# Order of two weight loads at the head of a decode kernel: the last 64 rows of wq ahead of the other 512

## The chip, the cores and the metric

The kernel runs on one core of one Trainium2 chip. The metric is the device time of one execution in microseconds (us). Profiles are single executions taken by the hardware profiler; positions in them are us from the start of the profiled span, which is some 1.8 us shorter than the device time (378.4 against 380.22 in the profiled run of before).

## The reference

One decode step of a transformer block, four sequences of one token, width 576:

```python
q = (layernorm(x) @ wq)                 # wq: 576 x 4096, 32 heads of 128
k, v = last 4096 positions of 16 cached heads, each used by two query heads
h  = x + softmax(q k / sqrt(128)) v @ wo
h2 = h + (relu(gate(ln(h))) * up(ln(h))) @ W_down     # hidden width 4608
```

The caches make up most of the traffic: 4 sequences x 16 cached heads, four heads to a tile, so 16 K tiles and 16 V tiles of 4 MB each. Inputs and output are bf16.

## The kernel before

All large loads are issued by SyncE, in one list, and go to one DMA queue. K and V tiles and the main part of wq share a ring of four 4 MB slots. A load waits only for the last reader of the cells that it overwrites.

```python
def main_rows(W):                       # 512 rows: 128 partitions x 32 KB, one run each
    return W[0:512, :].rearrange("(p r) n -> p (r n)", r=4)

def last_rows(W):                       # 64 rows: 128 partitions x 4 KB, 512 KB in one piece
    return W[512:576, :].rearrange("r (a n) -> (r a) n", a=2)

s = ring_slot()
wq_off = slot0 + s * TILE
place(("wq", 0), wq_off, TILE, "QMM",
      lambda e: e.dma_start(out=arena[:, wq_off:wq_off + TILE], in_=main_rows(A_wq)), key=f"slot{s}")
P.dma("sync", ("L", "wq", 1), lambda e: e.dma_start(out=pT[:, 0:2048], in_=last_rows(A_wq)), "d_wq1")
for g in range(NTILE):
    add_kv("K", g)
    if g >= 4:
        add_kv("V", g - 4)
# ... the last V tiles, wo, gate, up and down weights
```

The q projection takes the main part first (chunks 0 to 3) and the last rows as chunk 4, so the wait for the last rows is met late:

```python
def pe_q():
    for c in range(DC):                 # 5 chunks of the contraction
        ...
                deps = []
                if bk == g == 0:
                    deps = {0: [("L", "wq", 0), "xnT", "c_xnT"], 4: [("L", "wq", 1)]}.get(c, [])
```

What follows of q: two evictions, which are copies of matmul results out of TensorE's result memory (L407, L408; 2.43 and 2.42 us), then transposes on TensorE, and eight copies on ScalarE (L422) that spread q into the operand of the QK matmuls (L455). A K tile is first transposed in place by VectorE (L431, two halves). The fourth K tile takes the ring slot of wq, so its load waits for the q matmuls.

The down projection ends the kernel: groups of 18 matmuls (L713), the last of them as the last pieces of W_down land.

Of the kernel before, what the change touches and what calls it, by code (L numbers as in the profile page):

```python
# [122 lines left out]
def bass_sequential_preLN__sliding_block_cached__glu_gated_reglu__decode_kernel(  # L123
# [12 lines left out]
    with ExitStack() as es:  # L136
# [5 lines left out]
        P = Prog()  # L142
# [54 lines left out]
        pT = pp[:, 0:4096]  # L197
# [34 lines left out]
        def ring_slot():  # L232
            s = ring[0] % NSLOT
            ring[0] += 1
            return s
# [12 lines left out]
        def main_rows(W):  # L248
            return W[0:512, :].rearrange("(p r) n -> p (r n)", r=4)

        def last_rows(W):
            return W[512:576, :].rearrange("r (a n) -> (r a) n", a=2)

        s = ring_slot()
        wq_off = slot0 + s * TILE
        place(("wq", 0), wq_off, TILE, "QMM",
              lambda e: e.dma_start(out=arena[:, wq_off:wq_off + TILE], in_=main_rows(A_wq)), key=f"slot{s}")
        P.dma("sync", ("L", "wq", 1), lambda e: e.dma_start(out=pT[:, 0:2048], in_=last_rows(A_wq)), "d_wq1")
        for g in range(NTILE):
            add_kv("K", g)  # L260
            if g >= 4:
# [21 lines left out]
        for j in range(4):  # L283
            wd_off.append(off)
            for r0, r1 in ((0, 9),) if j < 3 else ((0, 6), (6, 8), (8, 9)):
                place(("wd", j, r0), off + r0 * D, (r1 - r0) * D, ("DOWN", 1),
                      lambda e, off=off, j=j, r0=r0, r1=r1: e.dma_start(  # L287
                          out=arena[:, off + r0 * D:off + r1 * D],
                          in_=B_W_down[j * 1152:(j + 1) * 1152, :].rearrange("(p r) n -> p (r n)", p=128)[:, r0 * D:r1 * D]))
# [18 lines left out]
                                                in_=c_qm[:, :, :].rearrange("p q (h j) -> p q h j", j=4),  # L308
# [4 lines left out]
                                                in_=to_v[:, :, :].rearrange("p n (k a) -> p n k a", a=4),  # L313
# [303 lines left out]
        for a in range(8):  # L617
            for n in range(2):
                for j in range(4):
# [4 lines left out]
                    else:  # L624
# [6 lines left out]
                                             in_=bass.AP(tensor=psb, offset=512 + 224, ap=[[4096, 128], [1, 64], [0, 2]])), ["part1"])  # L631
# [87 lines left out]
        for n in range(2):  # L719
            P.dma(("sync", "scalar")[n], ("O", n), lambda e, n=n: e.dma_start(  # L720
                out=orow[:, 288 * n:288 * n + 288], in_=bass.AP(tensor=out_sb, offset=32 * n * 288, ap=[[8 * 288, 4], [1, 288]])),
# [31 lines left out]
```

## Time and profile before

| what | value |
|---|---|
| time, median of the 3 runs | 380.82 us (380.12 to 381.21) |
| span of the profiled run | 378.4 us |
| moved | 159.76 MB, 422 GB/s on average |
| DMA's share of the chain of waits | 61% |

The page of before. The row of digits is the busy share of the 16 DMA engines in 40 equal slices of the span, in tenths (9 is 90% or more); the queue's line has packets, MB, and the share of 16 engines' span; the last line is the chain of work that ended last, by engine.

```profile
span 378.4 us, 2668 instructions
...
DMA  8999999999999999999999999999999999999994
...
DMA packets 6660, 159.76 MB, mean 422 GB/s; under 512 B 748, under 2 KB 888, under 8 KB 1528
...
q1 hardware_dynamic: 6632, 159.59, 98.4%
...
DMA 61%; PE 19%; DVE 15%; issue 4%; SPq 1%
```

The DMA engines are busy from end to end on one queue. The time is set by how early this stream opens, how fast it runs and how soon its slowest engine is through; compute is on the path only at the very end (the time is the last landing plus 5.06 to 5.20 us while the clock stays at 1.00, see *All together*). The chain's last line still gives PE and DVE 34%: they free the ring slots that later loads wait for (SyncE's K and V loads waited 251.9 us in total for the matmuls of L34). Those loads are issued behind a backlog (the shortest time from issue to landing of a K tile was 17.9 us, with a tile landing every 9.71 us), and the stream does not stop for them: the DMA digit is 9 in 38 of 40 slices.

The timeline of before, its opening. Columns: start, duration, engine and line, operation, tiles; in brackets the idle time before it and what ended it.

```profile
0.73 0.38 SPq L257 DMA_DIRECT2D sb_arena<-in_A_wq_dram  x1
...
1.18 0.41 SPq L258 DMA_DIRECT2D sb_pp<-in_A_wq_dram  x1
...
1.63 35.71 SPq L245 DMA_DIRECT2D sb_arena<-in_A_k_cache_dram  x5
...
12.98 0.62 PE L387 MATMUL psb<-sb_arena,sb_xnT 128*32 128x512 bf16 x4 [4.23 <-DMA sb_arena<-in_A_wq_dram]
...
17.06 2.43 ACT L407 CAST sb_pp<-psb 128x512 bf16<-128x512 f32 x1 [8.51 <-PE psb L387]
...
20.80 9.69 ACT L422 COPY sb_arena<-sb_q_keep 32x256 bf16<-32x256 bf16 x8
...
23.96 8.77 DVE L431 STREAM_TRANSPOSE sb_arena<-sb_arena 128x4096 f32<-128x4096 f32 x2 [2.38 <-DMA sb_arena<-in_A_k_cache_dram]
...
32.79 0.66 PE L455 MATMUL psb<-sb_arena 128*32 128x512 bf16 x4 [12.63 <-DVE sb_arena L431]
```

Read it as a race: the first QK matmul (32.79) was released by the transposes of the first K tile, while the q copies had ended at 20.80 + 9.69 = 30.49. So q had 2.3 us to spare.

The DMA issues of before, us from issue to landing in the last column:

```profile
sb_arena<-in_A_wq_dram SPq DMA_DIRECT2D x1, 4096.0 KB, 12.2
...
sb_pp<-in_A_wq_dram SPq DMA_DIRECT2D x1, 512.0 KB, 13.0
```

### The profile page before, as it was taken

The page shows a single profiled execution, that of the slowest core. Times are in us where ns is not written, and L with a number is a line of the kernel's source. Part 1 is how long each engine was busy: PE and PEld are TensorE (multiplying, and loading weights), DVE is VectorE, ACT ScalarE, POOL GpSimd, SP SyncE. Part 2 cuts the span into 40 slices and gives each one's busy share as a digit, 9 for nine tenths or more (in the row PEclk, how much of TensorE's full clock was granted, in tenths as well). Part 3 has the DMA queues.
Part 4 walks back from the last instruction along what each step waited for, and adds up shares of the span by engine and source line. Part 5 has one row for each costly group of instructions (what it writes and reads, how often), then busy time and mean ns, then how long its engine had stood idle before and what let it go on. Part 6 is the DMA issues. An engine that isn't in the chain of part 4 may idle for free.

```text
span 378.4 us, 2668 instructions
## 1 busy us (share of the span) xinstructions
PE 213.3 (56%) x1471; PEld 38.3 (10%) x703; DVE 230.6 (61%) x206; ACT 54.2 (14%) x89; POOL 21.9 (6%) x44
## 2 busy tenths in 40 slices
PE   0404443149919191739291935674746598876774
PEld 0000000001101010101010100010101010003322
DVE  3178989779392959593838777766568523343220
ACT  3192000301000113010101130101010500122010
POOL 8860000000000000000000000000000000000000
PEclk9955888759958697687788895968796988998689
DMA  8999999999999999999999999999999999999994
GB/s 333 443 441 429 414 433 440 443 426 416 435 434 443 423 421 436 436 440 419 423 436 436 436 423 429 435 436 433 423 429 438 429 436 423 441 421 422 416 426 190
DMA packets 6660, 159.76 MB, mean 422 GB/s; under 512 B 748, under 2 KB 888, under 8 KB 1528
## 3 DMA queue, kind: packets, MB, share of 16 engines
q1 hardware_dynamic: 6632, 159.59, 98.4%
q8 instruction: 8, 0.13, 0.1%
q14 instruction: 4, 0.03, 0.0%
q10 hardware_dynamic: 16, 0.01, 0.0%
HBM read 159.58 MB, written 0.00 MB: 422 GB/s over the span
## 4 chain that ended last, share of the span: by engine, by line
DMA 61%; PE 19%; DVE 15%; issue 4%; SPq 1%
DMA sb_arena<-in_A_k_cache_dram 52%; DVE sb_arena L431 13%; PE psb L34 11%; DMA sb_arena<-in_B_W_down_dram 9%; PE psb L455 4%; PE psb L519 3%; DVE sb_o_tmp L532 1%; DVE sb_pp L497 1%; PE psb L545 0%; PE psb L713 0%; SPq L245 0%; PE psb L486 0%; SPq L287 0%; DVE sb_fq L543 0%; DVE sb_out_sb L716 0%
## 5 line engine op out<-in xcount | busy, mean ns | idle before, releaser
L431 DVE STREAM_TRANSPOSE sb_arena<-sb_arena 128x4096 f32<-128x4096 f32 x32 | 140.7, 4429 | 63.8 <-DMA sb_arena<-in_A_k_cache_dram 63.8
L34 PE MATMUL psb<-sb_arena,sb_pp 128*128 128x512 bf16 x384 | 106.6, 387 | 0.0
L455 PE MATMUL psb<-sb_arena 128*32 128x512 bf16 x256 | 44.3, 639 | 107.3 <-DVE sb_arena L431 107.3
L519 PE MATMUL psb<-sb_arena,sb_pp 128*128 128x512 bf16 x128 | 50.2, 392 | 9.3 <-DVE sb_o_tmp L532 9.3
L34 PE MATMUL psb<-sb_arena 128*32 128x512 bf16 x256 | 45.1, 643 | 0.0
L529 ACT COPY sb_o_tmp<-psb 32x512 f32<-32x512 f32 x32 | 18.5, 577 | 182.8 <-PE psb L34 182.5
L532 DVE TENSOR_TENSOR sb_o_tmp<-psb,sb_fm 32x512 f32<-32x512 f32 x32 | 21.7, 678 | 18.6 <-PE psb L34 18.1
L455 PEld LDWEIGHTS psb<-sb_arena 128*32 128x32 bf16 x256 | 9.7, 118 | 150.0 <-DVE sb_arena L431 120.2
L519 PEld LDWEIGHTS psb<-sb_arena,sb_pp 128*128 128x128 bf16 x128 | 12.7, 99 | 115.0 <-issue 115.0
L536 DVE TENSOR_REDUCE sb_o_sel<-sb_o_tmp 128x128 f32<-128x512 f32 x16 | 17.7, 1104 | 0.5
L476 ACT ACTIVATE sb_pp<-psb,sb_stat 128x512 bf16<-128x512 f32 x8 | 5.4, 682 | 80.9 <-DVE sb_stat L471 80.9
L497 DVE TENSOR_SCALAR sb_pp<-psb,sb_m 128x512 bf16<-128x512 f32 x16 | 10.8, 738 | 4.6 <-PE psb L486 4.6
L329 POOL TENSOR_SCALAR_AFFINE_SELECT sb_toq<-sb_toq 128x128 f32<-128x128 f32 x16 | 12.6, 788 | 2.3
L500 ACT ACTIVATE sb_pp<-psb,sb_m 128x512 bf16<-128x512 f32 x16 | 9.8, 697 | 12.7 <-PE psb L486 12.7
L535 DVE TENSOR_TENSOR sb_o_tmp<-sb_o_tmp,sb_fm 64x512 f32<-64x512 f32 x16 | 11.0, 690 | 0.5
L422 ACT COPY sb_arena<-sb_q_keep 32x256 bf16<-32x256 bf16 x8 | 9.7, 1445 | 0.1
L545 PE MATMUL psb<-sb_fq,sb_toq 128*128 128x4 f32 x8 | 1.8, 301 | 12.2 <-DVE sb_fq L543 12.2
L486 PE MATMUL psb<-sb_pp,sb_to_v 128*32 128x256 bf16 x64 | 4.3, 403 | 6.0 <-DVE sb_pp L480 6.0
L480 DVE STREAM_TRANSPOSE sb_pp<-sb_pp 128x512 bf16<-128x512 bf16 x8 | 5.5, 712 | 3.4 <-ACT sb_pp L476 3.4
L408 DVE CAST sb_pp<-psb 128x512 bf16<-128x512 f32 x1 | 2.4, 2425 | 8.1 <-PE psb L387 8.1
L713 PE MATMUL psb<-sb_arena,sb_pp 128*32 128x288 bf16 x72 | 5.9, 319 | 2.6 <-DMA sb_arena<-in_B_W_down_dram 2.6
L684 DVE TENSOR_TENSOR sb_pp<-psb,sb_pp 128x384 bf16<-128x384 f32 x3 | 1.5, 551 | 8.4 <-PE psb L675 8.4
(126 smaller groups left out, 91.6 us busy)
## 6 DMA issues: line engine op xcount, KB each, us to landing
sb_arena<-in_A_k_cache_dram SPq DMA_DIRECT2D x16, 4096.0 KB, 26.0
sb_arena<-in_A_v_cache_dram SPq DMA_DIRECT2D x16, 4096.0 KB, 27.9
sb_arena<-in_A_wo_dram SPq DMA_DIRECT2D x1, 4608.0 KB, 26.3
sb_arena<-in_B_W_gate_dram SPq DMA_DIRECT2D x1, 4608.0 KB, 27.8
sb_arena<-in_A_wq_dram SPq DMA_DIRECT2D x1, 4096.0 KB, 12.2
sb_arena<-in_B_W_down_dram SPq DMA_DIRECT2D x3, 1296.0 KB, 31.9
sb_arena<-in_B_W_up_dram SPq DMA_DIRECT2D x1, 3456.0 KB, 28.8
sb_arena<-in_B_W_up_dram SPq DMA_DIRECT2D x1, 1152.0 KB, 31.2
```

The lines of the kernel that those rows point to most:

```text
L34: return e.add_instruction(mybir.InstMatmult(name=e.bass.get_next_instruction_name(), engine=mybir.EngineType.PE, ins=[e.lower_ap(rhs), e. ...
L329: pool(f"c_toq{q + 1}", lambda e, q=q: e.affine_select(out=toq[:, :, :, :], in_=toq[:, :, :, :], pattern=[[0, 16], [-32, 4], [-1, 2]], com ...
L422: act("QW", lambda e, i=i, q=q: e.copy(out=bass.AP(tensor=arena, offset=32 * i * AW + 2 * i + q, ap=[[AW, 32], [512, 16], [136, 4], [32, 4]]),
L431: dve(("TRA", g, w), lambda e: e.transpose(out=dst, in_=src), [("L", "K", g)] if w == 0 else [])
L455: fn = lambda e, out_=out_, lhsT=lhsT, rhs=rhs, start=start, stop=stop: e.matmul(out_, lhsT=lhsT, rhs=rhs, start=start, stop=stop, skip_gr ...
L497: dve(("EV", b, 1), lambda e, out_=out_, src=src, a=a: e.tensor_scalar(out=out_, in0=src, scalar1=m4[:, a:a + 1], scalar2=None, op0=ALU.mu ...
L500: act(("EV", b, 0), lambda e, out_=out_, src=src, a=a: e.activation(out=out_, in_=src, func=ACT.Copy, scale=m4[:, a:a + 1]), deps + (["c_m ...
L519: fn = lambda e, lhsT=lhsT, rhs=rhs, k=k, j=j: e.matmul(bank[2 + j], lhsT=lhsT, rhs=rhs, start=(k == 0), stop=(k == 7), skip_group_check=True)
L529: act(("OSC", g), lambda e, j=j: e.copy(out=o_tmp[32 * j:32 * j + 32, 0:512], in_=bank[2 + j][32 * j:32 * j + 32, :]), [("PV", g), ("OSEL" ...
L532: dve(("OSD", g), lambda e, j=j: e.tensor_tensor(out=ot(32 * j, 32), in0=bank[2 + j][32 * j:32 * j + 32, :].rearrange("p (t d) -> p t d", ...
L535: dve(("OS", g), lambda e: e.tensor_tensor(out=ot(64, 64), in0=ot(64, 64), in1=fmb(64, 64), op=ALU.mult), [("OSC", g)])
L536: dve(("OSEL", g), lambda e: e.tensor_reduce(out=o_sel[:, qd, b, :], in_=o_tmp[:, 0:512].rearrange("p (t d) -> p d t", d=DH), axis=AX.X, o ...
```

## The change

The load of the last 64 rows is issued ahead of the main part. The aim of such a change would be to have the small piece there before it is needed; nothing else differs, and the instructions of every engine but SyncE stand in the same order.

```diff
+        P.dma("sync", ("L", "wq", 1), lambda e: e.dma_start(out=pT[:, 0:2048], in_=last_rows(A_wq)), "d_wq1")
         s = ring_slot()
         wq_off = slot0 + s * TILE
         place(("wq", 0), wq_off, TILE, "QMM",
               lambda e: e.dma_start(out=arena[:, wq_off:wq_off + TILE], in_=main_rows(A_wq)), key=f"slot{s}")
-        P.dma("sync", ("L", "wq", 1), lambda e: e.dma_start(out=pT[:, 0:2048], in_=last_rows(A_wq)), "d_wq1")
         for g in range(NTILE):
```

## The prediction

> **What bounds the kernel.** The DMA stream. The page counts 159.76 MB over a span of 378.4 us, 422 GB/s on average, and its row of DMA digits is 9 in 38 of 40 slices. Nearly all is one queue (98.4% of 16 engines' span), fed by SyncE. The semaphore events of the loads show a 4 MB tile landing every 9.71 us, from 23.94 us (first K tile) to 326.47 us (last V tile). DMA holds 61% of the chain of waits. The four-slot ring keeps a backlog: the shortest time from issue to landing of a K tile is 17.9 us against some 9.7 us of transfer, so about 8 us of other loads stand before it even at the worst.
>
> **What the change does.** No instruction and no byte is removed or added. On SyncE's queue two neighbours swap: the 0.5 MB load of the last 64 rows (128 packets of 4 KB) goes before the 4 MB load of the other 512 rows (128 packets of 32 KB). Neither waits for anything, each has its own semaphore, and the first K tile is third in both orders.
>
> [...] the main part landed at 12.94 us, the small part at 14.21 (1.27 us later, its own transfer), the first K tile at 23.94.
>
> So now the small part should land at about 4 us and the main part at about 14.2, where the pair ended before. TensorE starts the q projection with the main part, at 12.98 us before; it should start at about 14.2. In before the small part landed under the first matmuls and cost no wait (its chunk started at 16.37), so nothing is won in return. All that follows moves by about 1.25 us, an estimate from these landings: q evictions from 17.06 to about 18.3, the end of ScalarE's eight q copies (9.69 us) from 30.49 to about 31.75.
>
> **How much is critical.** None. (1) The first QK matmul at 32.79 waits for the transposes of the first K tile (VectorE, 8.77 us from 23.96), not for the q copies: 2.3 us of slack, 1.25 used. (2) VectorE idles 2.38 us before that transpose; its small q operations end at about 22.8 instead of 21.6. (3) The fourth K load reuses the q weights' slot and waits for the q matmuls (13.8 us in the queue's waits); it goes from about 17.4 to 18.6 us, but the loads ahead of it last until 43.78.
>
> A second-order term is the start: the first 32 KB packets took 1.6 to 2.2 us instead of the later 1.21. With 4 KB packets first this may change by a few tenths, either sign; I put it at zero.
>
> **Prediction: 380.8 us**, 379.7 to 381.9 in 8 of 10 cases. Chances: faster by over 2%: 0.01; within 2%: 0.98; slower by over 2%: 0.01.
>
> **What would show the steps.** Right: the q matmuls wait about 1.25 us longer for the q weights; the first QK matmul still at 32.8, still released by the transpose; the first K tile landing within 0.4 us of 23.9, all later landings within 0.5 us; same bytes. Wrong: first QK released by ScalarE; a hole in the DMA rate in the first slices; a K landing shifted by over 1 us.
>
> **What would make it wrong.** If 4 KB packets at the very start run much slower than at 13 us[...], the whole stream shifts by that hole[...]. If the q copies slowed down, the 1 us of slack left could go; even then the backlog should absorb it.

The forecast's sum is the median of the three known runs of before, 380.82 us, plus nothing: every term, the second-order one of the start included, was put at zero.

## The result, and the profile after

| | before | after |
|---|---|---|
| median | 380.54 us (4 runs, 380.12 to 381.21) | 379.72 us (4 runs, 379.70 to 379.77) |
| span of the profiled run | 378.4 us | 377.9 us |

The ratio was 0.9977, with a 95% interval of 0.9960 to 0.9994. Of those four times of before, 380.82 and 381.21 are of a long kind that e1_null explains below, and none of the four of after is; so the 0.82 us between the medians is partly luck. Ratios here are the mean time of one kernel's fast runs over that of the other's of the same rounds, so not quite the ratio of the medians quoted. The interval excludes 1, and 379.72 lies 1.1 us under the predicted 380.8, at the very edge of the range (0.02 us inside it).

The page of after:

```profile
span 377.9 us, 2668 instructions
...
DMA  8999999999999999999999999999999999999994
...
DMA packets 6660, 159.76 MB, mean 423 GB/s; under 512 B 748, under 2 KB 888, under 8 KB 1528
...
q1 hardware_dynamic: 6632, 159.59, 98.4%
...
DMA 61%; PE 18%; DVE 15%; issue 4%; SPq 1%
```

Same packets and bytes. The timeline of after, its opening:

```profile
0.74 0.39 SPq L254 DMA_DIRECT2D sb_pp<-in_A_wq_dram  x1
...
1.19 0.41 SPq L258 DMA_DIRECT2D sb_arena<-in_A_wq_dram  x1
...
1.64 35.18 SPq L245 DMA_DIRECT2D sb_arena<-in_A_k_cache_dram  x5
...
13.93 0.62 PE L387 MATMUL psb<-sb_arena,sb_xnT 128*32 128x512 bf16 x4 [6.38 <-DMA sb_arena<-in_A_wq_dram]
...
18.01 2.43 ACT L407 CAST sb_pp<-psb 128x512 bf16<-128x512 f32 x1 [11.35 <-PE psb L387]
...
21.86 9.75 ACT L422 COPY sb_arena<-sb_q_keep 32x256 bf16<-32x256 bf16 x8
...
23.62 8.77 DVE L431 STREAM_TRANSPOSE sb_arena<-sb_arena 128x4096 f32<-128x4096 f32 x2 [0.98 <-DMA sb_arena<-in_A_k_cache_dram]
...
32.45 0.62 PE L455 MATMUL psb<-sb_arena 128*32 128x512 bf16 x4 [11.23 <-DVE sb_arena L431]
```

The q matmuls start 0.95 us later, and the q copies end at 31.61 instead of 30.49. But the first K tile is there 0.34 us *earlier* (23.62 against 23.96), and so is the first QK matmul, still released by the transposes. The DMA issues of after:

```profile
sb_arena<-in_A_wq_dram SPq DMA_DIRECT2D x1, 4096.0 KB, 12.7
...
sb_pp<-in_A_wq_dram SPq DMA_DIRECT2D x1, 512.0 KB, 3.4
```

The last weights landed on the slowest of the 16 engines at 374.52 us instead of 375.07. So the stream moved, not the compute.

To see the opening, I took the trace's DMA packet records and worked out a *lag*: the time now, minus the time that the bytes finished by now would take at the full rate (16 engines x 32768 B per 1.2125 us, 432 GB/s). A stream that runs at full rate has a constant lag. (Packets under way count in proportion.)

```
lag (us) at        2.5    3.0    3.5    4.0    5.0    8.0   23.0 us
before            2.13   2.31   2.48   2.60   2.61   2.61   2.61
after             2.26   2.34   2.39   2.42   2.47   2.49   2.47
```

The difference arises in the first 4 us. After 23 us both lags grow alike, to 4.25 us in before and 4.08 in after at 370 us. In before each engine's first packet is one of 32 KB, which took 1.57 to 2.25 us; once the stream runs, such a packet takes 1.21 us. In after the stream opens with 4 KB packets; the first sixteen took 0.16 to 0.49 us each, and soon 0.159, and the first sixteen 32 KB packets behind them took 1.21 to 1.50 us.

### The profile page after: what moved, and what is told of

It is laid out like the page before. It is cut to its first block, busy times and chain, and to the rows that moved or that the text cites. A ratio compares the mean times of both kernels' runs of the same rounds, so it can differ in the third digit from the quotient of the medians.

```text
span 377.9 us, 2668 instructions
## 1 busy us (share of the span) xinstructions
PE 212.0 (56%) x1471; PEld 38.5 (10%) x703; DVE 231.3 (61%) x206; ACT 54.2 (14%) x89; POOL 21.8 (6%) x44
## 4 chain that ended last, share of the span: by engine, by line
DMA 61%; PE 18%; DVE 15%; issue 4%; SPq 1%
DMA sb_arena<-in_A_k_cache_dram 52%; DVE sb_arena L431 13%; PE psb L34 11%; DMA sb_arena<-in_B_W_down_dram 9%; PE psb L455 4%; PE psb L519 3%; DVE sb_o_tmp L532 1%; DVE sb_pp L497 1%; PE psb L545 0%; PE psb L713 0%; SPq L245 0%; PE psb L486 0%; SPq L287 0%; DVE sb_fq L543 0%; DVE sb_out_sb L716 0%
## 5 line engine op out<-in xcount | busy, mean ns | idle before, releaser
L34 PE MATMUL psb<-sb_arena,sb_pp 128*128 128x512 bf16 x384 | 105.4, 384 | 0.0
L455 PE MATMUL psb<-sb_arena 128*32 128x512 bf16 x256 | 42.5, 631 | 106.3 <-DVE sb_arena L431 106.3
L519 PE MATMUL psb<-sb_arena,sb_pp 128*128 128x512 bf16 x128 | 49.6, 387 | 9.3 <-DVE sb_o_tmp L532 9.3
L34 PE MATMUL psb<-sb_arena 128*32 128x512 bf16 x256 | 43.6, 641 | 0.0
```

Of the source, the lines that this page charges most:

```text
L34: return e.add_instruction(mybir.InstMatmult(name=e.bass.get_next_instruction_name(), engine=mybir.EngineType.PE, ins=[e.lower_ap(rhs), e. ...
L455: fn = lambda e, out_=out_, lhsT=lhsT, rhs=rhs, start=start, stop=stop: e.matmul(out_, lhsT=lhsT, rhs=rhs, start=start, stop=stop, skip_gr ...
L519: fn = lambda e, lhsT=lhsT, rhs=rhs, k=k, j=j: e.matmul(bank[2 + j], lhsT=lhsT, rhs=rhs, start=(k == 0), stop=(k == 7), skip_group_check=True)
```

## The experiments

The theories.

- **A**: the packets that open the stream set its lag; small ones open it better.
- **B**: what counts is the order of the two real parts of wq, through the matmuls behind them.
- **C**: chance: each execution draws its own lag and time.
- **D**, formed after the first four runs: A's gain is real but small, and beside it some executions of either kernel are about 1 us longer at the end. Times without that extra microsecond are called undisturbed below.

Five of the sixteen runs below were the kernel before itself or its change again, because the effect is so small. All runs gave correct outputs; the dummy loads and dummy matmuls touch only cells that nothing reads before they are overwritten.

### e1_null: before against itself

No edit.

> The kernel before against itself. Every theory expects a ratio of 1.000; the interval shows how small a difference these rounds can tell. Theory A (the first packets' size sets how late the slowest DMA engine enters the stream) expects the last of the 16 engines to land the first K tile at 23.9 us again (within 0.1), and the first of them at 23.35. Theory C (chance: each execution draws its own lag) expects that landing to differ from 23.94 by some tenths, and the time to scatter over about 1 us as the four runs of before did (380.12 to 381.21).

Measured: ratio 1.0004 (0.9992 to 1.0017), median 380.19 us. First K tile complete at 23.92 us, lag at 8 us 2.67. So the opening repeats, against C. The times: four between 379.93 and 380.38 and one of 381.17, which was the profiled one. That last one shows where the microsecond is. Windows of e1_null: length, busy time and instructions (x) of each engine, then the granted TensorE clock (PEclk, the share of its full clock that TensorE was given), the DMA share and GB/s.

```profile
core 0: us, PE busy (x) PEld busy (x) DVE busy (x) ACT busy (x) POOL busy (x), PEclk, DMA share, GB/s
...
372.00:374.00 2.00, 1.23 (x18) 0.77 (x18) 0.00 (x0) 0.00 (x0) 0.00 (x0) 0.82 0.67 263
374.00:376.90 2.90, 2.35 (x18) 1.23 (x18) 0.45 (x1) 0.39 (x1) 0.00 (x0) 0.50 0.03 12
```

The same stretch of before:

```profile
374.00:376.00 2.00, 1.36 (x18) 0.75 (x18) 0.45 (x1) 0.39 (x1) 0.00 (x0) 1.00 0.04 13
```

The last 18 matmuls took 2.35 us at a granted clock of 0.50 and 1.36 us at 1.00. This group stands behind the last load, so the 0.99 us goes straight into the time.

### e2_again: the changed kernel again

No edit.

> The changed kernel once more. Theory A: ratio about 0.998 (0.997 to 0.999), first K tile complete at 23.6 us within 0.1, the spread between the first and the last of the 16 engines at that landing about 0.3 us, against 0.6 in before. Theory C: ratio 1.000 within the null run's interval, and a first K landing anywhere between 23.5 and 24.0.

Measured: ratio 1.0000 (0.9986 to 1.0013), times 379.54, 379.71, 379.79, 380.87, 380.88. First K tile at 23.71, spread over the engines 0.44 us (A had expected 23.6 within 0.1, and 0.3), lag 2.46. The ratio alone says that there is no gain; the trace says that the stream opened early again. Two of five runs were of the long kind, against none of nine of before in these rounds, and that hid the gain in the mean.

### e3_split4 and e13_split4: the old order, opened by 4 KB packets

```diff
+        QA = 2048
+        P.dma("sync", ("L", "wqa"), lambda e: e.dma_start(out=arena[:, wq_off:wq_off + QA], in_=main_rows(A_wq)[:, 0:QA]), "d_wqa")
         place(("wq", 0), wq_off, TILE, "QMM",
-              ... out=arena[:, wq_off:wq_off + TILE], in_=main_rows(A_wq) ...
+              ... out=arena[:, wq_off + QA:wq_off + TILE], in_=main_rows(A_wq)[:, QA:TILE] ...
```

The first q matmul waits for both pieces.

> The order of before, but the first 4 KB of each partition of the main part are a DMA of their own, so the stream opens with 128 packets of 4 KB and continues with packets of 28 KB. Theory A (small packets at the start): same gain as the change, first K tile complete at 23.6 us, ratio about 0.998, although the last 64 rows still come after the main part. Theory B (it is the order of the two parts of wq that matters, for instance because the matmuls and all behind them move by 1 us): no gain, first K tile at 23.9, ratio 1.000. Theory C: 1.000.

Measured: 1.0001 (0.9987 to 1.0015), times 379.71 to 381.07; first K tile at 24.03, lag at 8 us 2.58. A's number failed: the gain in lag was less than half, and no time was won. This trace lost another 0.37 us between 30 and 60 us, where the other traces lost 0.06 to 0.19. So the run was repeated later:

> The split run once more. So far 2.58 us of lag at 8 us and undisturbed times of 379.7 to 380.3, between the two kernels. If 4 KB packets at the opening are enough, the lag is 2.4 to 2.5 us and undisturbed times fall to 379.7; if packets 32 KB apart open more slowly than contiguous ones, 2.55 to 2.65 and 380.0 again.

Measured: 0.9991 (0.9975 to 1.0008); lag 2.53; undisturbed times 379.85 to 380.04, against 379.78 to 380.12 for before in the same rounds, so no gain in time is shown. First packets of this kind took 0.17 to 0.94 us in the first run, more than the contiguous ones of after. Small packets help the lag, but 32 KB apart they helped less here (2.58 and 2.53 us, against 2.42 to 2.49 for the changed kernel and 2.61 to 2.67 for before).

### e4_split16: two halves of 16 KB packets

The same edit with `QA = 8192`.

> The order of before, the main part as two DMAs of 16 KB packets. Theory A expects part of the gain or none: first K tile complete at about 23.75 us (between 23.6 and 23.95), ratio 0.999. A variant of A in which it is the small transfer and not the small packet that counts expects none, as the first transfer is 2 MB: 23.9 us. Theories B and C: 1.000.

Measured: 1.0003 (0.9990 to 1.0015), first K tile at 23.87, lag 2.68: no gain.

### e5_again: the changed kernel a third time

> The changed kernel a third time. Theory D (what the first runs showed so far): the stream really opens 0.2 us earlier on the average engine and ends 0.4 to 0.6 us earlier on the slowest, and beside it one run in five is about 1.05 us longer because TensorE is granted half its clock in the last 3 us. D expects two groups of times, 379.5 to 379.9 and, where the end is slow, 380.7 to 381.0, the median at 379.7, and first K tile complete at 23.6 to 23.75 us. Theory C (no effect at all): median 380.1, first K tile complete near 23.9.

Measured: median 379.81; five times from 379.51 to 380.16 and one of 380.95, which was the profiled one and again had half the clock at its end. First K tile at 23.84 on the slowest engine, a little later than expected; lag 2.46. This trace then lost 0.42 us between 30 and 100 us, where before lost 0.24, so that at 370 us its lag was 4.23, nearly that of before (4.25). The ratio was 0.9975 (0.9958 to 0.9992), but here seven of eleven runs of before were of the long kind (380.99 to 381.55). The same pair of kernels thus gave 1.0000 on one chip and 0.9975 on another.

### e6_precontig, e15_precontig, e7_prestrided, e14_prestrided: a dummy load in front

```diff
+        P.dma("sync", ("L", "pre"), lambda e: e.dma_start(out=pT[:, 2048:4096], in_=SRC), "d_pre")
         place(("wq", 0), wq_off, TILE, "QMM",
```

`SRC` is `last_rows(A_wq)` (contiguous) or `main_rows(A_wq)[:, 0:2048]` (4 KB of every 32 KB). The real loads follow in the old order, and the first q matmul also waits for the dummy.

> Before with a dummy load of the same contiguous 512 KB in front, 128 packets of 4 KB, into cells that nobody reads; the real loads follow in the order of before. The time grows by the 0.5 MB it adds, about 1.2 us. The measure here is how far the stream lags behind its full rate once it runs (bytes completed by 8 us against 432 GB/s): 2.61 and 2.67 us in before, 2.49 and 2.46 in the changed kernel. If the first packets of contiguous 4 KB are what helps: 2.4 to 2.5 us. If it is the order of the two real parts: 2.6 to 2.7.

> The same dummy load, but its 128 packets of 4 KB are taken 32 KB apart (the first 4 KB of each partition of the main part), as in the split run that won nothing. If packet size alone sets the lag: 2.4 to 2.5 us at 8 us, as in the contiguous one. If the addresses count: 2.55 to 2.65, as in the split run (2.58).

> The dummy load of contiguous 4 KB packets again: 2.41 us of lag the first time; 2.4 to 2.5 expected by both.

> The dummy load of strided 4 KB packets again: 2.49 us of lag the first time. Packet size alone: 2.4 to 2.5 again, equal to the contiguous dummy run. Addresses: above the contiguous run by 0.05 to 0.1 again.

Measured lag at 8 us: contiguous 2.41 and 2.34; strided 2.49 and 2.52. The times were 380.89 and 381.76, and 381.02 and 381.20, one run each, with the 0.5 MB more. The old order with a stranger in front opens as early as the changed kernel: B is out. As an estimate, less the 1.21 us that 0.5 MB take at the 432 GB/s above, e6 comes to 379.68 us and e7 and e14 to 379.81 and 379.99, against undisturbed medians of 379.71 (change) and 380.06 (before) in the table below; in e15 the clock fell to half at the end, which accounts for its longer time (the fall cost 0.99 us in e1_null against before). Strided packets come out between.

### e8_warm: a tiny load in front

```diff
+        P.dma("sync", ("L", "warm"), lambda e: e.dma_start(out=pT[:, 2048:2304], in_=main_rows(A_wq)[:, 0:256]), "d_warm")
```

> Before with a tiny load in front, 128 packets of 512 B (64 KB in all, 0.15 us of transfer). If the loss is a first-use cost of each engine, whatever the packet, the tiny packets take it and the 32 KB packets behind them run at 1.21 us from the start: lag at most 2.5 us. If it belongs to 32 KB packets that start together on 16 engines, they are as slow as before (1.6 to 2.2 us each) and the lag is 2.6 or more.

Measured: lag 3.17 us, 380.58 us in one run. A first-use cost that any packet could pay is not it: the first sixteen 32 KB packets behind the 64 KB took 1.32 to 2.30 us, no better than in before, and they started one issue later. As the tiny packets were nearly through before the big ones came (two to six packets under way from 2.2 to 2.4 us), a cost that returns after a pause is not excluded.

### e9_null and e10_again: the pair once more, on one chip

> The kernel before against itself, on the chip and in the rounds of the other three. Ratio 1.000 within the interval; two groups of times, about 380.1 and, where the end is slow, 381.0 to 381.5; the stream's lag at 8 us 2.6 to 2.7 us as in the two traces so far.

Measured: ratio 1.0005 (0.9989 to 1.0021); three times from 379.91 to 380.14 and three from 380.96 to 381.23; lag 2.66.

> The changed kernel a fourth time. Theory D: its group of undisturbed times lies at 379.7, 0.3 to 0.5 us under that of before in the same rounds; lag at 8 us 2.4 to 2.5 us. Theory C: both groups coincide.

Measured: ratio 0.9983 (0.9970 to 0.9995); six times from 379.57 to 380.16, none long, median 379.60, against 379.91 to 380.20, median 380.03, for the undisturbed runs of before and e9_null in the same rounds; lag 2.42.

### e11_lastlate: the last rows moved the other way

```diff
-        P.dma("sync", ("L", "wq", 1), ... last_rows(A_wq) ...)
         for g in range(NTILE):
             add_kv("K", g)
+            if g == 0:
+                P.dma("sync", ("L", "wq", 1), ... last_rows(A_wq) ...)
```

> Before, with the last 64 rows moved the other way, behind the first K tile. The q matmuls can then end only at about 25 us, the q copies at about 38.5, and the first QK matmul starts there, 6 us later than in before and now released by ScalarE. If the place of q in the stream is off the critical path by the width that the prediction claims (the queue holds other loads till 43.8 us), the time is that of before: undisturbed 380.1, ratio 1.000, the last V tile landing at 326.5 within 0.4. If the q path mattered to the change's effect, this run is slower by 1 us or more. Its opening is that of before: lag at 8 us 2.6 to 2.7.

Measured: ratio 0.9996 (0.9982 to 1.0010); undisturbed times 379.90 to 380.33 and one of 381.00; last V tile at 326.51; lag 2.66. The timeline of e11_lastlate (its lines are one further down than those of before):

```profile
23.94 1.05 PE L388 MATMUL psb<-sb_pp,sb_xnT 128*32 128x512 bf16 x8 [7.37 <-DMA sb_pp<-in_A_wq_dram]
...
28.47 9.74 ACT L423 COPY sb_arena<-sb_q_keep 32x256 bf16<-32x256 bf16 x8
...
38.35 0.62 PE L456 MATMUL psb<-sb_arena 128*32 128x512 bf16 x4 [10.53 <-ACT sb_arena L423]
```

The first QK matmul came 5.6 us later than in before and was now released by the q copies, and the time did not move. The q path has at least that much room, so the 1.1 us that the change takes of it cost nothing.

### e12_fill: dummy matmuls to hold the clock

On top of the changed kernel:

```diff
             wv = arena[:, wd_off[j]:wd_off[j] + WDJ].rearrange("p (r n) -> p r n", n=D)
+            for _ in range((0, 0, 12, 6)[j]):
+                pe(None, lambda e: e.matmul(bank[2][0:32, 0:288], lhsT=hhT[:, 0:32], rhs=arena[:, wd_off[0]:wd_off[0] + 288],
+                                            start=True, stop=True, skip_group_check=True))
```

> The changed kernel with 12 and 6 matmuls of no use (into a bank that nobody reads) ahead of the last two groups of the down projection, where TensorE waits for weights anyway. If the slow ends come from TensorE being too idle[...] before the last 18 matmuls, they become rarer or vanish: all times at 379.6 to 379.9, none at 380.8 or over, ratio to before 0.998 or lower. If the clock falls whatever TensorE does there, slow ends stay at one in five or more, and the time is that of the changed kernel.

Measured: ratio 0.9996 (0.9980 to 1.0013), median 380.37, times 379.66 to 381.02. It failed as a better version. In its trace the clock stayed at 1.00 from 374 to 376 us, and no span of its six runs was longer than 378.7 us, against 379.0 or more in the long runs of the other kernels. But its profiled run took 380.8 us with a span of 377.9: 2.9 us over the span instead of 1.8, and its run of 381.02 had a span of 378.6. In that trace an instruction fetch of 16 KB, the ninth (before has eight), ended at 381.0 us, after the output. Whether the fetch is what the run waited for was not tried. Other runs had spans of 378.4 to 378.7. So the filler may hold the clock (one trace does not show it), but the kernel with it was not faster.

### e16_all4: 4 KB packets throughout the main part

The old order, the main part as two loads of 2 MB, each `[128, 4, 2048]`, so that every packet has 4 KB.

> The order of before, the main part as two loads of 2 MB whose packets are all 4 KB (8 KB apart). If small packets open the stream better, the lag at 4 us is 2.35 to 2.5 against 2.60 to 2.65 in before; it then creeps up by about 0.04 us per 8 packets because a 4 KB packet takes 159 ns, not 1213/8 = 152, to about 2.8 at 13 us.

Measured: lag 2.98 us at 4 us and 3.33 at 13 us; 380.54 us in one run. A miss: the first packet started at 2.18 us instead of about 1.75, and the lag grew faster. Here a first load of 512 small packets opened worse than one of 128 (2.42 us at 4 us in after). The later start goes in part with the issue: SyncE's instruction for the first load took 0.67 us (0.74 to 1.41) instead of 0.38 in before (0.73 to 1.11). Why the packets then came later still is open.

### All together

Lag at 8 us, by what opens the stream:

```
4 KB packets of one contiguous 512 KB   2.49 2.46 2.46 2.42 2.48 (changed kernel, e12), 2.41 2.34 (dummy)
4 KB packets, 32 KB apart, 512 KB       2.58 2.53 (split), 2.49 2.52 (dummy)
32 KB packets                           2.61 2.67 2.66 2.66 (before twice more, e11)
16 KB packets                           2.68
```

The two other openings were worse: 64 KB of 512 B packets 3.17 us (e8_warm), 2 MB of 4 KB packets 3.12 (e16_all4). Over the four traces of the 32 KB line the first sixteen packets took 1.22 to 2.25 us each, against 1.21 later.

What was lost at the head was not made up in any trace, though a gain there can be lost again on the way (e5_again). At 370 us the lags were 4.25, 4.30, 4.29 and 4.30 for the 32 KB openings in the order above, 4.08, 4.01, 4.23 (e5_again) and 4.01 for the changed kernel, 4.04 and 3.96 for the contiguous dummy, and 4.10 and 4.15 for the strided one. The end of the stream then sets the time: in the twelve traces whose clock stayed at 1.00 at the end, the time is the landing of the last weights on the slowest engine plus 5.06 to 5.20 us; in the five whose clock fell, plus 6.04 to 6.16 us. Only e12_fill, with its late fetch, stands apart (6.23 us, clock at 1.00).

Times, all timed runs of both kernels (the separate profiled run of before, 380.22, is not among them), split at a gap in which no run of either lies (380.38 to 380.82):

```
          runs   under the gap: count, median (range)        over the gap: count, median
before     57    36, 380.06 (379.77 to 380.38)               21, 381.06
after      21    18, 379.71 (379.51 to 380.16)                3, 380.88
```

Every profiled run of these two kernels that lies over the gap (e1_null, e5_again, e9_null) shows the clock at 0.50 from 374 to 376 us; every one under it shows 1.00. Under the gap the change wins 0.35 us, 0.09%. The split was made after the times were seen, and pools chips. Within each of the four sets of rounds that ran both kernels, the medians under the gap differ by 0.32 to 0.48 us, always in favour of the change. The share over the gap is 21 of 57 and 3 of 21; as it went from none of nine to seven of eleven for the same kernel on two chips, no claim is made that the change alters it.

## Why the prediction was right or wrong

- *"What bounds the kernel. The DMA stream."* Right. The time followed the lag of the stream, and not a q path made 5.6 us later (e11_lastlate).
- *"(1) The first QK matmul ... waits for the transposes"*, 1.25 us of slack used. Right in kind: it was released by the transposes at 32.45. The q matmuls came 0.95 us later and not 1.25, because the whole pair of loads was through earlier (the main part at 13.88 us; the pair ended at 14.21 in before). TensorE's wait before them grew by 2.15 us (4.23 to 6.38), as the small load of x, too, landed earlier (3.75 us instead of 5.64) and the normalisation was done sooner; the prediction did not have this, and nothing on the path depends on it.
- *"(3) The fourth K load ... but the loads ahead of it last until 43.78."* Right: in e11_lastlate the q matmuls end at 25 us, and the last V tile lands at 326.51 against 326.47.
- *"A second-order term is the start ... I put it at zero."* **This is the step that failed**: a term that was named and then set to zero, while it measured 0.35 us of undisturbed time. The text saw that the first 32 KB packets were slow and did not follow it up. Opening with contiguous 4 KB packets took about 0.2 us off the lag at 8 us (2.61 to 2.67 against 2.42 to 2.49), and in three of four traces of the change most of this was still there at 370 us. The first K tile landed 0.34 us earlier, inside the 0.4 that the prediction allowed; the last weights landed 0.55 us earlier, outside its 0.5. The same gain in lag came from a dummy load in front of the old order, so it is the opening and not the place of the last rows.
- *"Prediction: 380.8 us"*, centred on the median of three runs. Two of those three (380.82 and 381.21) lie over the gap; the undisturbed median of before is 380.06. So 0.7 us of the 1.1 us of error, the larger part, was in the starting point, and the range was laid around a mixture of two groups. Which group those runs fell into was luck; that the times fall into groups could have been asked before.
- *"the main part landed at 12.94 us, the small part at 14.21 ..., the first K tile at 23.94"*: three loads that landed in the order of issue, and the forecast took it that they would do so in the new order. They did: the small part landed at 4.18 us, the main part at 13.88, the first K tile at 23.60. Nor was there a hole between the two parts of wq: the last 4 KB packet ended at 3.82 us, and the first sixteen 32 KB packets started at 3.48 to 3.82.

What stays open: why the sixteen 32 KB packets that opened the stream together were slow (1.57 to 2.25 us in before, against 1.21 later), and why contiguous 4 KB packets opened better than spread ones (2.34 to 2.49 us of lag against 2.49 to 2.58). The size of the packets and the size of the load were not separated: every opening that helped was a load of 512 KB in 4 KB packets, and no 512 KB load with larger packets was tried. Also open is why the time gained is 0.35 us where the mean lag gained 0.2. The traces show that the slowest engine's last landing moved more (375.07, 375.02 and 374.80 in before; 374.52, 374.34, 374.80 and 374.41 in after) than the mean of the 16 engines (373.82 to 373.87; 373.57 to 373.79). Instruction fetches of 16 KB, eight in before and eight in after, took 0.95 to 1.11 us each on the way (46 to 364 us) and may have a part in it; that was not tested.

The long runs are explained as far as this: TensorE ran its last 18 matmuls at half clock, in 2.35 us at 0.50 (e1_null) against 1.36 at 1.00 (before); the other stretches of half clock were not costed. In the clock records of all traces here every whole stretch of constant clock is 3.41 us or a multiple of it (40 stretches in before, 3.41 to 27.3 us; 36 in after, 3.41 to 34.1), and the stretches lie differently in each execution: the stretch of full clock in which the last 18 matmuls ran began at 368.70 us in before and at 367.78 in after. Idleness alone does not decide: from 370 to 372 us TensorE was busy for 0.27 us in e5_again, where the clock fell, and for 0.18 us in before, where it did not. What separates the 18 traces is the last boundary before the last weights landed, when the stretches are laid out as a grid of 3.41 us. In the five traces where the clock fell there (boundaries at 373.06 to 374.15 us), TensorE had been busy for 1.28 to 1.56 us of the 3.41 us before it; in the 13 where it stayed at 1.00, for 1.59 (before) to 3.06 us. The most is e12_fill, whose boundary, at 373.38 us, lay where others fell. That the position of this boundary decides fits all traces, but is inference and not shown: the margin is thin, the ends of matmuls are modelled in these profiles, and no run moved the boundary on purpose.

## What to carry to other kernels

In a kernel bound by one DMA stream, look at the first packets: here what the stream lost while it opened stayed lost (lag 2.61 us at 8 us and at 23 us in before), and a load of 512 KB in contiguous 4 KB packets in front opened it a little earlier, by about 0.2 us. Here this paid only with a load that is needed anyway; a dummy costs its own bytes, an estimated 1.21 us from 0.5 MB at 432 GB/s (e6_precontig took 380.89 us in one run). Before predicting tenths of a per cent, look at how single times are grouped: a median of three can sit in the wrong group, and a ratio of means can read 1.0000 or 0.9975 for the same pair. A term that the profile shows (first packets of 2 us instead of 1.2) should be sized by its effect on the bound, not set to zero because its sign is unknown.
